# A sum of the down product copied by ScalarE and added by GpSimd, and two attention products put back to their even places

## The chip, the cores and the metric

The kernel runs on one core of a Trainium2 chip. The metric is the device time of one execution in microseconds (us); the number shown is the median of three runs. A core has TensorE (matrix products, PE in the profile, with its weight loads as PEld), VectorE (DVE), ScalarE (ACT), GpSimd (POOL) and SyncE (SP), which here issues the transfers. Each engine has an instruction stream of its own.

## The reference

Everything is in float32. The input x has 2048 tokens of 576 features. A layer norm is followed by two branches that read the same normalised input: a 32-head attention and a gated feed-forward network with 4608 hidden columns. Their results are multiplied and added to x.

```python
x  = A_x                                   # 1 x 2048 x 576
xn = (x - mean) / sqrt(var + 1e-5)
s  = softmax(q k^T * 18**-0.5) v @ wo      # 32 heads of 18, q, k, v = xn @ wqkv
f  = (gelu(xn @ w_gate) * (xn @ w_up)) @ w_down
return x + s * silu(f)
```

## The kernel before, in words

**Sections and rounds.** The feed-forward work is cut into 4 blocks of 512 tokens (index `b`) and 36 groups of 128 hidden columns, so 144 *sections*, run by `section`. Two sections (`g` = 0 and 1) make a *round* `r`, which covers 256 hidden columns; there are 18 rounds in a block. A section makes gate and up sums in one PSUM tile `pgu` from 27 pairs of products (`wh`, `wl` are the high and low halves of a weight, split by GpSimd at lines 118 and 120). ScalarE applies gelu (line 429), VectorE multiplies by the up sum (line 432), and the results `h` are split into `ah` and `al` by GpSimd.

**Attention in the slots.** From section 11 on, a section also carries eight attention *slots*. A slot issues a score product `pe` (line 887), which ScalarE reads with an exponential into `pT` (line 888), and a product `pm` (line 846) that VectorE reduces to row maxima `mx` (line 847) for scores that are needed later. `spread` puts these 16 pairs of products between the 27 pairs of `pgu`, evenly, at places `i * 27 // 16 + 1`. After the section TensorE multiplies `pT` with the values (`acc`, line 904).

**The down product.** After the `g` = 0 section of a round comes the down product of the round before (`downs`, `down`), in a form with seven products instead of eight. Each of the seven sums goes through a PSUM tile `py` (lines 513 to 518). `halved` issues each in two halves, the second one after the first half of the next sum; the last two halves, of the sixth and of the seventh sum, stand next to each other. `take` then adds `py` to the running sum `M[m]`; VectorE does this for all seven (line 568). In the first round of a block (`r` = 0) it is a copy (lines 564 and 566). The order of the seven is `PRODUCTS`, whose last but one entry is `(4, (5, 1))`: it makes `M[4]`, from part 1 of the weight tile `T`.

**The ring.** `pgu`, `pe`, `pm`, `acc` and `py` share a ring of four PSUM tiles of two banks each, given out in turn. `pgu` holds one for the whole section, so the slots go round the other three. With the tiles numbered by the order in which the down product fills them, the fifth, sixth and seventh `py` are followed by the first `pe`, the first `pm` and the second `pe`; after that the second `pm` takes the tile of the first `pe`, the third `pe` that of the first `pm`, the third `pm` that of the second `pe`, and so on.

**Rounds that form T.** `T` holds the weights of the down product, split into high and low halves, in seven combinations. In 18 of the rounds (`FORMED`) it is computed: GpSimd makes the sums `tsum` from the raw weights, ScalarE writes the high halves (`high_b`, lines 488, 490 and 491), GpSimd the low ones (`low_b`, lines 496, 498 and 499), and the result is stored to memory; later rounds load it from there. There is one `T`, so line 488, which writes parts 3 to 6, waits for the first four of the seven products to have read them, line 490 (part 2) for the fifth, and line 491 (parts 0 and 1) for the last.

**What sets the order.** The instruction order of TensorE and of SyncE's queue is that of the program. The scheduler sets the order of the other engines, except for instructions that are held to program order (`keep_in_program_order`).

**LATER.** A section that follows a down product passes `LATER = {1: 1, 4: 1}` to `spread`: entry 1 (the first `pm`) and entry 4 (the third `pe`) of the 16 stand one pair of `pgu` later than their even places.

Of the kernel before, what the change touches and what calls it, by code (L numbers as in the profile page):

```python
# [8 lines left out]
F32 = mybir.dt.float32  # L9
F32R = mybir.dt.float32r  # L10
AF = mybir.ActivationFunctionType
ALU = mybir.AluOpType
# [5 lines left out]
P = 128  # L18
# [14 lines left out]
SLOTS = 8  # L33
# [6 lines left out]
NF = NB * NR * G  # L40
# [5 lines left out]
DC, TH = D // 2, TB // 2  # L46
ENDS = NF - len(FIRST) - NU * NA
# [4 lines left out]
SCALED = G * (NR + PLAIN + 1) - len(FIRST) + 1  # L52
PRODUCTS = ((2, (0, 6)), (5, (1, 3)), (3, (2, 5)), (6, (3, 4)), (0, (4, 2)), (4, (5, 1)), (1, (6, 0)))
SHARED = 8
LATER = {1: 1, 4: 1}
QUARTERS = ((0, 0, 6), (0, 1, 4), (1, 0, 1), (1, 1, 5))
PIECES = ((0, 3, 7), (0, 0, 3), (1, 3, 7), (1, 0, 3))
ADD, SUB = ALU.add, ALU.subtract
# [14 lines left out]
    return ap.bitcast(F32)  # L73


def spread(pairs, specials, first=None, hooks={}, later={}):

    n, m = len(pairs), len(specials)
    at = [-(-(i + 1) * n // m) - 1 if first is None else i * n // m + first + later.get(i, 0) for i in range(m)]
    out = []  # L80
    for i in range(n):
        out += [p for p, j in zip(specials, at) if i == j] + hooks.get(i, [])
        out.append(pairs[i])
    return out
# [3 lines left out]
def kernel(ctx: ExitStack, tc: tile.TileContext, x, wqkv, wo, w_gate, w_up, w_down, out):  # L88
    nc = tc.nc
# [83 lines left out]
    with tc.tile_pool(name="pro", bufs=1) as pro, tc.tile_pool(name="pps", bufs=1, space=PSUM) as pps:  # L173
# [120 lines left out]
        def split_qk(t, raw):  # L294
            hi, lo = (pro.tile([P, KT, P], F32R, name=f"q{m}{t}") for m in "hl")
            first = split(hi, lo, raw)
            put_qk(t, hi, lo)
            return first
# [31 lines left out]
        t = ORDER[0]  # L330
# [24 lines left out]
        for b in range(NB):  # L355
            if b == NB - 1:
                tc.keep_in_program_order(nc.scalar.activation(eps, eps, AF.Tanh))
            for n, t in enumerate(ORDER):
# [4 lines left out]
                if b == 0 and ahead_qk:  # L363
                    first = split_qk(*ahead_qk.pop(0))
# [28 lines left out]
    ffn = ctx.enter_context(tc.tile_pool(name="ffn", bufs=1, reuse_waits="tile"))  # L393
# [3 lines left out]
    FF = {"w": ahead, "xd": XD, "down": [], "gates": [], "n": 0, "hooks": {}, "raw": {},  # L397
          "M": ffn.tile([P, 7, 2, DC], F32, name="M"),
          "A": [ffn.tile([P, 7, TH], F32R, name=m) for m in ("ah", "al")],
          "T": ffn.tile([P, 2, 7, DC], F32R, name="T")}  # L400
# [4 lines left out]
    def ring(name):  # L405

        return ps.tile([P, 2, TB], F32, name=name, tag="ring", bufs=RING)
# [135 lines left out]
    def down_plain():  # L543
        (ah, al), M = FF["A"], FF["M"]
        jobs = []
        for i, c, into in ((0, 0, ((6, ALU.add),)), (0, 1, ((2, ALU.add), (5, ALU.subtract))),
                           (1, 0, ((3, ALU.subtract), (6, ALU.subtract))), (1, 1, ((5, ALU.add),))):

            def add_to(py, into=into):
                for m, op in into:  # L550
                    nc.vector.tensor_tensor(M[:, m], M[:, m], py[:, :, 0:DC], op=op)

            jobs.append(([(h, 2 * g + i, w, 2 * g + c) for g in range(G) for h, w in ((ah, 0), (ah, 1), (al, 0))], add_to))
        halved(jobs)

    def down(b, r, then={}):
        if b == 0 and r < PLAIN:
            return down_plain()
        (ah, al), T, M = FF["A"], FF["T"], FF["M"]

        def take(py, m):
            if r == 0:
                if b == 1:
                    nc.vector.tensor_copy(M[:, m], py[:, :, 0:DC])
                else:
                    nc.scalar.activation(M[:, m], py[:, :, 0:DC], AF.Copy)
            else:
                nc.vector.tensor_tensor(M[:, m], py[:, :, 0:DC], M[:, m], op=ALU.add)  # L568
            for eng, to, op, by in then.get(m, ()):
                eng.tensor_tensor(M[:, to], M[:, to], M[:, by], op=op)  # L570

        terms = ((ah, 0), (ah, 1), (al, 0))
        if FF["n"] < NF - ENDS:
            halved([([(h, i, w, k) for h, w in terms], lambda py, m=m: take(py, m)) for m, (i, k) in PRODUCTS])
        else:
            for m, (i, k) in PRODUCTS:
                py = ring("py")
                for t in range(2):
                    tt = slice(t * P, (t + 1) * P)
                    for n, (h, w) in enumerate(terms):  # L580
                        nc.tensor.matmul(py[:, t, 0:DC], h[:, i, tt], T[:, w, k], start=n == 0, stop=n == 2)  # L581
                take(py, m)
        if r == NR - 1 and b < NB - 1:
            FF["gates"].append(b)
            for k, (p, q) in enumerate(COMBINED):
                combine_at(6 * k + 6, nc.gpsimd, q)
                combine_at(6 * k + 6, nc.gpsimd, p)

    def combine_at(i, eng, what):
        FF["hooks"].setdefault(i, []).append(lambda: combine(eng, *what))  # L590
# [15 lines left out]
        FF["rawd"] = ffn.tile([P, G, D], F32, name="rawd")  # L606
        nc.sync.dma_start(FF["rawd"], w_down[r * G * P:(r + 1) * G * P, :].rearrange("(g p) n -> p g n", p=P))

    def section(specials=(), slots=False, later={}):

        n = FF["n"]
        FF["n"] += 1
        b, r = divmod(n // G, NR)
        g = n % G
        keep = tc.keep_in_program_order
        pairs, pg, pu = gate_up()
        hooks, FF["hooks"] = FF["hooks"], {}

        def hook(i, what):
            hooks.setdefault(i, []).append(what)  # L620

        for i in range(n + 1, min(n + 3, NF)):
            if i not in FF["raw"]:
                FF["raw"][i] = load_gu(gu_part(i))
        nxt = FF["raw"].pop(n + 1, None)
        one = split_ap if n + 1 < ATT.start else split
        if nxt:
            for k in range(NG - 1):
                split_gu(nxt, k, one)
        if n == 0:  # L630
            load_rawd(0)
        if g == 0 and (b, r) in FORMED:
            raw = FF["rawd"]
            hook(12, lambda: sums_b(raw))
        new = n + 1 < NF and (n + 1) % (NR * G) == 0
        xd = []
        if new:
            for k in range(NG - 1):
                hook(9 * k + 9, lambda k=k: xd.append(load_xd(b + 1, k)))
        for p in spread(pairs, specials, 1 if slots else None, hooks, later):  # L640
            p()
        if nxt:
            split_gu(nxt, NG - 1, one)
        if n == 0:
            cut_plain_b(FF["rawd"])
        FF["w"] = nxt
        FF["act"] = activate(pg, pu, g, n)
        if new:
            xd.append(load_xd(b + 1, NG - 1))
            for t in hooks.get(len(pairs), ()):  # L650
                t()
            FF["xd"] = xd

    def downs(then={}):
        done = False
        while FF["down"] and (FF["down"][0][-1] < FF["n"] or FF["n"] == NF):
            down(*FF["down"].pop(0)[:-1], then)
            done = True
        return done

    def finish():

# [123 lines left out]
    with tc.tile_pool(name="att", bufs=1, reuse_waits="tile") as att:  # L786
# [103 lines left out]
        def slot_pairs(s):  # L890

            um, im = divmod(s + LEAD, NS)
            return [lambda: score_pair(*divmod(s, NS))] + [lambda: max_pair(um, im)] * (um < NU)
# [64 lines left out]
            downs()  # L958
            finish()
        scaled = gated = 0  # L960
        later = {}
        for n in range(NU * NA):
            u, i = divmod(n, NA)
            s0 = n * SLOTS
            section([p for s in range(s0, s0 + SLOTS) for p in slot_pairs(s)], True, later)
            load_k(n + KB)
            if i == 1 and u + 2 < NU:
                load_q(u + 2)
            gates()
            tasks(n, 0)  # L970
            if FF["n"] % G == 1 and SCALED <= n < NU * NA - 2 and 2 < FF["n"] % (NR * G) < NR * G - 2:
                done = scaled + gated
                if (scaled + 1) * NA + 4 < n:
                    jobs, k = (load_scale, scale, store_scale), scaled
                    scaled += 1
                else:
                    jobs, k = (load_gate, gate, store_gate), gated
                    gated += 1
                jobs[0](k, done % 2)
                at(n + 2, 0, jobs[1], k, done % 2)  # L980
                at(n + 3, 0, jobs[2], k, done % 2)
            um, im = divmod(s0 + LEAD + SLOTS, NS)
            for kt in range(i * SLOTS // 2, (i + 1) * SLOTS // 2):
                values(u, kt)
            if im == 0 and um <= NU:
                max_parts(um - 1)
            load_v(n + 2)
            tasks(n, 1)
            later = LATER if downs() else {}
            tasks(n, 2)  # L990
            finish()
            for b in range(2):
                if n == NU * NA - NA + 2 * b:
                    load_o(b)
# [3 lines left out]
    with tc.tile_pool(name="epi", bufs=1, reuse_waits="tile") as epi:  # L998
# [7 lines left out]
        n = 0  # L1006
# [133 lines left out]
        first = FF["n"]  # L1140
# [37 lines left out]
        for m in ("rawd", "tsum"):  # L1178
            t = ffn.tile([P, 2, D], F32, name="xxs", tag=m)
# [16 lines left out]
        M = FF["M"]  # L1196
# [17 lines left out]
        for i, c, m in QUARTERS:  # L1214
            t = ffn.tile([P, 2, DC], F32, name="tg", tag=("h0", "h1")[c], bufs=2 - c)
# [34 lines left out]
```

## Time and profile before

| what | value |
|---|---|
| median of three runs | 2529.95 us (2529.44 to 2530.23) |
| the profiled execution: its time | 2528.7 us |
| its span from first to last instruction | 2526.9 us |
| granted TensorE clock, mean | 1.000 |
| busy: TensorE, weight loads, VectorE, ScalarE, GpSimd | 100%, 72%, 75%, 66%, 63% |

The busy time of TensorE overlaps itself, because the products of the two halves of the array run side by side and their ends are modelled; so 100% says that TensorE nearly always has a product under way, not that it runs as densely as it could. Where it loses time is read from the distance between the starts of its products. In the waits, PEld is TensorE's weight load: a wait there is a loss only in so far as the product behind it starts late.

### The profile page before, as it was taken

To read this page: it belongs to the slowest core of one execution; us is meant where nothing else is said; L and a number is where in the kernel's file an instruction comes from. 1 tells how busy PE (TensorE), PEld (TensorE's weight loads), DVE (VectorE), ACT (ScalarE), POOL (GpSimd) and SP (SyncE) were. 2 spreads that over 40 slices of the span, in tenths; PEclk is the share of its full clock that TensorE was granted. 3 is DMA by queue.
4 is the path that set the end of the run, shared out by engine and by line. 5 is a ranking of instruction groups with operands and counts; after the bars stand their busy time and mean duration, and the time that the engine had idled before them with its cause. 6 is when DMAs were issued, how large, how long until landed. Compare 5 with 4: busy or idle time off the path is not lost.

```text
span 2526.9 us, 58757 instructions
## 1 busy us (share of the span) xinstructions
PE 2520.1 (100%) x23434; PEld 1827.4 (72%) x23434; DVE 1890.4 (75%) x2085; ACT 1666.2 (66%) x1889; POOL 1599.4 (63%) x1652
## 2 busy tenths in 40 slices
PE   9999999999999999999999999999999999999999
PEld 8888866666766677666667666676666676666789
DVE  5326788888888888888887888888887788888247
ACT  3223377778777776777777777677777777777731
POOL 3005688888888875666657556566667666666773
PEclk9999999999999999999999999999999999999999
DMA  8965456555585566666677666666668666665766
GB/s 262 313 206 139 120 173 170 153 168 164 170 246 155 165 177 151 167 163 168 169 218 191 175 174 166 169 170 163 156 162 244 167 173 173 172 164 153 190 186 243
DMA packets 416649, 455.40 MB, mean 180 GB/s; under 512 B 109428, under 2 KB 289396, under 8 KB 416376
## 3 DMA queue, kind: packets, MB, share of 16 engines
q1 hardware_dynamic: 416376, 451.64, 65.1%
q8 instruction: 186, 3.05, 0.5%
q14 instruction: 87, 0.71, 0.1%
HBM read 354.38 MB, written 97.13 MB: 179 GB/s over the span
## 4 chain that ended last, share of the span: by engine, by line
PE 97%; DMA 2%; DVE 1%; POOL 0%; issue 0%; SPq 0%; ACT 0%; POOLq 0%; DVEq 0%
PE pgu L420 35%; PE acc L904 18%; PE py L518 16%; PE pm L846 10%; PE pe L887 9%; PE po L194 7%; PE po L1059 1%; DMA raw<-in_B_w_up_dram 1%; PE py L581 1%; PE pt L264 0%; DMA rT<-rec 0%; DMA xx<-in_A_wo_dram 0%; DMA T<-ts 0%; DMA xx<-in_A_x_dram 0%; DVE ol L1042 0%
## 5 line engine op out<-in xcount | busy, mean ns | idle before, releaser
L888 ACT ACTIVATE pT<-pe 128x1024 f32<-128x1024 f32 x1024 | 1048.6, 1027 | 469.4 <-PE pe L887 435.6
L847 DVE TENSOR_REDUCE mx<-pm 128x2 f32<-128x1024 f32 x1024 | 1218.7, 1226 | 143.9 <-PE pm L846 128.8
L420 PE MATMUL pgu<-xd,wh 64*128 64x512 f32 x5184 | 958.5, 393 | 0.0
L420 PEld LDWEIGHTS pgu<-xd,wh 64*128 64x128 f32 x5184 | 496.2, 184 | 122.5 <-issue 41.6
L118 POOL TENSOR_SCALAR wh<-raw 128x384 fp32r<-128x384 f32 x402 | 208.5, 519 | 506.7 <-PE pgu L420 264.0
L420 PE MATMUL pgu<-xd,wl 64*128 64x512 f32 x2592 | 514.4, 390 | 0.2 <-POOL wl L120 0.2
L904 PE MATMUL acc<-pT,VS 128*32 128x512 f32 x4096 | 466.0, 595 | 0.0
L120 POOL TENSOR_TENSOR wl<-raw,wh 128x384 fp32r<-128x384 f32 x402 | 407.4, 1014 | 33.0
L846 PE MATMUL pm<-KA,QT 64*128 64x512 f32 x2048 | 411.9, 396 | 0.2 <-DVE mx L847 0.2
L887 PE MATMUL pe<-QT,KA 64*128 64x512 f32 x2048 | 408.1, 391 | 0.0
L518 PE MATMUL py<-T,ah 64*128 64x288 f32 x3848 | 389.8, 294 | 0.0
L568 DVE TENSOR_TENSOR M<-py,M 128x576 f32<-128x576 f32 x448 | 333.2, 756 | 54.7 <-PE py L518 39.9
L518 PEld LDWEIGHTS py<-T,ah 64*128 64x128 f32 x3848 | 317.6, 184 | 53.2 <-issue 52.8
L441 POOL TENSOR_TENSOR al<-h,ah 128x512 fp32r<-128x512 f32 (+1 forms) x143 | 295.6, 2067 | 49.2 <-ACT ah L438 24.0
L904 PEld LDWEIGHTS acc<-pT,VS 128*32 128x32 f32 x4096 | 120.0, 109 | 276.9 <-issue 229.8
L518 PE MATMUL py<-T,al 64*128 64x288 f32 x1924 | 294.9, 291 | 0.0
L420 PEld LDWEIGHTS pgu<-xd,wl 64*128 64x128 f32 x2592 | 247.6, 184 | 46.6 <-POOL wl L120 0.6
L887 PEld LDWEIGHTS pe<-QT,KA 64*128 64x128 f32 x2048 | 192.9, 184 | 112.0 <-DVE mx L847 12.5
L432 DVE TENSOR_TENSOR h<-h,pgu 128x512 f32<-128x512 f32 x139 | 95.6, 687 | 194.2 <-ACT h L429 190.1
L846 PEld LDWEIGHTS pm<-KA,QT 64*128 64x128 f32 x2048 | 195.1, 184 | 55.5 <-ACT pT L888 15.8
L518 PEld LDWEIGHTS py<-T,al 64*128 64x128 f32 x1924 | 192.2, 185 | 0.0
L429 ACT ACT_TABLE_LOAD x129 | 165.5, 1283 | 2.4
(151 smaller groups left out, 2138.4 us busy)
## 6 DMA issues: line engine op xcount, KB each, us to landing
T<-ts SPq DMA_DIRECT2D x98, 576.0 KB
KA<-qk SPq DMA_DIRECT2D x768, 72.0 KB
T<-ts SPq DMA_DIRECT2D x98, 432.0 KB
raw<-in_B_w_gate_dram SPq DMA_DIRECT2D x144, 288.0 KB
raw<-in_B_w_up_dram SPq DMA_DIRECT2D x144, 256.0 KB
ts<-T SPq DMA_DIRECT2D x36, 576.0 KB
VS<-vs SPq DMA_DIRECT2D x128, 152.0 KB
qk<-t SPq DMA_DIRECT2D x72, 256.0 KB
```

The lines of the kernel that those rows point to most:

```text
L118: first = nc.gpsimd.tensor_scalar(hi, raw, 1.0, 1.0, op0=ALU.mult, op1=ALU.mult)
L120: keep(nc.gpsimd.tensor_tensor(lo, raw, f(hi), op=ALU.subtract))
L194: nc.tensor.matmul(o, st, m, start=(i == 0), stop=(i == len(terms) - 1))
L420: nc.tensor.matmul(o, w[1 + wp][k][rr, c, :], xd[k][xp][rr, c, :], start=(i == 0), stop=(i == len(terms) - 1))
L441: low = two.tensor_tensor(lo, raw, f(hi), op=ALU.subtract)
L518: one = nc.tensor.matmul(py[:, t, 0:DC], h[rr, a, t * P:(t + 1) * P], T[rr, w, k], start=x == 0 and n == 0, stop=x == 1 and n == len(terms ...
L568: nc.vector.tensor_tensor(M[:, m], py[:, :, 0:DC], M[:, m], op=ALU.add)
L846: nc.tensor.matmul(pm[:, a], QS[u, r][rr, t * P:(t + 1) * P], KS[(u * NA + c) % KB][r][rr, :], start=True, stop=True)
L847: nc.vector.tensor_reduce(MX[u][:, 2 * r:2 * r + 2, t, c], pm, axis=AX.X, op=ALU.max)
L887: nc.tensor.matmul(pe[:, a], KS[(u * NA + c) % KB][r][rr, t * P:(t + 1) * P], QS[u, r][rr, :], start=True, stop=True)
L888: nc.scalar.activation(PT[u, kt][:, 2 * r:2 * r + 2, :], pe, AF.Exp, scale=SCALE)
L904: nc.tensor.matmul(ACC[u][32 * a:32 * a + 32, :], VS[(u * NA + c) % VB][:, v:v + 32], pt[:, a, :], start=first, stop=last, skip_group_chec ...
```

## The change

The sixth of a round's seven down sums (`MOVED`, that of `M[4]`) is no longer added by VectorE. ScalarE copies `py` into a tile `msum` in SBUF and GpSimd adds `msum` to `M[4]`. Both instructions are held to program order. This is done where `r > 0` and before the end rounds: 60 rounds. `msum` takes its place from the two buffers of the tag `h0`, which the `h` tiles of the `g` = 0 sections use. `LATER` and what passed it on are removed, so that the first `pm` and the third `pe` of the slots after a down product stand at their even places again.

```diff
-LATER = {1: 1, 4: 1}
+MOVED = PRODUCTS[-2][0]
...
-    at = [-(-(i + 1) * n // m) - 1 if first is None else i * n // m + first + later.get(i, 0) for i in range(m)]
+    at = [-(-(i + 1) * n // m) - 1 if first is None else i * n // m + first for i in range(m)]
...
         def take(py, m):
-            if r == 0:
+            if m == MOVED and r > 0 and FF["n"] < NF - ENDS:
+                t = ffn.tile([P, 2, DC], F32, name="msum", tag="h0", bufs=2)
+                tc.keep_in_program_order(nc.scalar.activation(t, py[:, :, 0:DC], AF.Copy))
+                tc.keep_in_program_order(nc.gpsimd.tensor_tensor(M[:, m], t, M[:, m], op=ALU.add))
+            elif r == 0:
...
-            section([p for s in range(s0, s0 + SLOTS) for p in slot_pairs(s)], True, later)
+            section([p for s in range(s0, s0 + SLOTS) for p in slot_pairs(s)], slots=True)
...
-            later = LATER if downs() else {}
+            downs()
```

The change shows in the instruction streams at two places. The first is a round that forms `T`: ScalarE's stream from the end of the `g` = 0 section (the last of the gelu's instructions, on `one_exp`) to the exponentials of the next section. Before:

```order
L431 ACTIVATE one_exp<-one_exp 128x1
L488 ACTIVATE T<-tsum 128x1152
L490 ACTIVATE T<-tsum 128x288
L491 ACTIVATE T<-rawd 128x576
L888 ACTIVATE pT<-pe 128x1024 x8
```

And now, with the copy at line 564:

```order
L431 ACTIVATE one_exp<-one_exp 128x1
L564 ACTIVATE msum<-py 128x576
L488 ACTIVATE T<-tsum 128x1152
L490 ACTIVATE T<-tsum 128x288
L491 ACTIVATE T<-rawd 128x576
L889 ACTIVATE pT<-pe 128x1024 x8
```

The copy of the sixth sum stands ahead of all three writes of `T`, and these stand ahead of the exponentials. Of the 60 copies, 16 are followed by line 488 in this way; in the other 44 rounds the next instruction is the exponential.

GpSimd's stream in the same kind of round, from the difference that makes `h` of the `g` = 0 section complete to the split of `h`, before:

```order
L449 TENSOR_TENSOR h_7230<-h_7230 128x256
L496 TENSOR_TENSOR T<-tsum,T 128x1152
L498 TENSOR_TENSOR T<-tsum,T 128x288
L499 TENSOR_TENSOR T<-rawd,T 128x576
L440 TENSOR_SCALAR ah<-h_7230 128x512
L441 TENSOR_TENSOR al<-h_7230,ah 128x512
```

And now:

```order
L449 TENSOR_TENSOR h_7244<-h_7244 128x256
L565 TENSOR_TENSOR M<-msum,M 128x576
L496 TENSOR_TENSOR T<-tsum,T 128x1152
L498 TENSOR_TENSOR T<-tsum,T 128x288
L499 TENSOR_TENSOR T<-rawd,T 128x576
L440 TENSOR_SCALAR ah<-h_7244 128x512
L441 TENSOR_TENSOR al<-h_7244,ah 128x512
```

The addition stands ahead of the low halves of `T`. In the other rounds it stands behind the split (line 441), ahead of the next section's weight splits.

The second place is TensorE's stream at the first slots of a section that follows a down product, from the second pair of `pgu` on (the first `pe` is behind the reader). Before:

```order
L420 MATMUL pgu<-xd_0_1008,wl 128x512 x2
L420 MATMUL pgu<-xd_0_1010,wh 128x512 x2
L846 MATMUL pm<-KA,QT_1954 128x512 x2
L420 MATMUL pgu<-xd_0_1008,wh 128x512 x2
L887 MATMUL pe<-QT_1953,KA 128x512 x2
L420 MATMUL pgu<-xd_0_1008,wl 128x512 x2
L420 MATMUL pgu<-xd_0_1010,wh 128x512 x2
L846 MATMUL pm<-KA,QT_1954 128x512 x2
L420 MATMUL pgu<-xd_0_1008,wh 128x512 x2
L420 MATMUL pgu<-xd_0_1008,wl 128x512 x2
L887 MATMUL pe<-QT_1953,KA 128x512 x2
L420 MATMUL pgu<-xd_0_1010,wh 128x512 x2
```

And now:

```order
L420 MATMUL pgu<-xd_0_1008,wl 128x512 x2
L847 MATMUL pm<-KA,QT_1954 128x512 x2
L420 MATMUL pgu<-xd_0_1010,wh 128x512 x2
L420 MATMUL pgu<-xd_0_1008,wh 128x512 x2
L888 MATMUL pe<-QT_1953,KA 128x512 x2
L420 MATMUL pgu<-xd_0_1008,wl 128x512 x2
L420 MATMUL pgu<-xd_0_1010,wh 128x512 x2
L847 MATMUL pm<-KA,QT_1954 128x512 x2
L420 MATMUL pgu<-xd_0_1008,wh 128x512 x2
L888 MATMUL pe<-QT_1953,KA 128x512 x2
L420 MATMUL pgu<-xd_0_1008,wl 128x512 x2
L420 MATMUL pgu<-xd_0_1010,wh 128x512 x2
```

The first `pm` and the third `pe` each moved ahead of one pair of `pgu`; the second `pe` and the second `pm` stayed. VectorE's stream changes only in that the additions of a down product (line 568, now 572) are six in a row instead of seven. SyncE's stream is the same.

More of the change, by code (lines that the diff above doesn't have):

```diff
@@ L73, in f, with spread @@
     return ap.bitcast(F32)
-def spread(pairs, specials, first=None, hooks={}, later={}):
+def spread(pairs, specials, first=None, hooks={}):
     n, m = len(pairs), len(specials)
-    at = [-(-(i + 1) * n // m) - 1 if first is None else i * n // m + first + later.get(i, 0) for i in range(m)]
+    at = [-(-(i + 1) * n // m) - 1 if first is None else i * n // m + first for i in range(m)]
     out = []
@@ L607, in load_rawd, with section @@
         nc.sync.dma_start(FF["rawd"], w_down[r * G * P:(r + 1) * G * P, :].rearrange("(g p) n -> p g n", p=P))
-    def section(specials=(), slots=False, later={}):
+    def section(specials=(), slots=False):
         n = FF["n"]
@@ L639, in section @@
                 hook(9 * k + 9, lambda k=k: xd.append(load_xd(b + 1, k)))
-        for p in spread(pairs, specials, 1 if slots else None, hooks, later):
+        for p in spread(pairs, specials, 1 if slots else None, hooks):
             p()
@@ L654, in downs @@
     def downs(then={}):
-        done = False
         while FF["down"] and (FF["down"][0][-1] < FF["n"] or FF["n"] == NF):
             down(*FF["down"].pop(0)[:-1], then)
-            done = True
-        return done
     def finish():
@@ L960 @@
         scaled = gated = 0
-        later = {}
         for n in range(NU * NA):
```

## Prediction

> **What bounds the kernel.** I read the page first, for the engine that sets the end, then the waits of the weight loads, since only those can hold TensorE up, and then two stretches of the timeline, because a sum over 2527 us mixes rounds of two kinds.
>
> ```profile
> PE 2520.1 (100%) x23434; PEld 1827.4 (72%) x23434; DVE 1890.4 (75%) x2085; ACT 1666.2 (66%) x1889; POOL 1599.4 (63%) x1652
> PE 97%; DMA 2%; DVE 1%; POOL 0%; issue 0%; SPq 0%; ACT 0%; POOLq 0%; DVEq 0%
> PEld acc L904 <- DVE mx L847: 45.3, 123, 0.4
> PEld pm L846 <- ACT pT L888: 15.8, 69, 0.4
> PEld pe L887 <- DVE mx L847: 12.5, 75, 0.2
> PEld pe L887 <- DVE M L568: 9.5, 58, 0.2
> ```
>
> The chain that ended last is TensorE for 97% of the span. So VectorE, ScalarE and GpSimd count only where TensorE waits for them, and all such waits of weight loads for the ring come to 83 us, of which a product hides most. The fourth row is the wait that the change removes; the second and third are those that could grow. Now a round without the forming of T, from its down product (first row) into the next section:
>
> ```profile
> 1525.39 0.54 PE L518 MATMUL py<-T,ah 64*128 64x288 f32 x4
> 1526.88 5.38 DVE L568 TENSOR_TENSOR M<-py,M 128x576 f32<-128x576 f32 x7 [0.66 <-PE py L518]
> 1531.02 0.41 PE L420 MATMUL pgu<-xd,wh 64*128 64x512 f32 x2
> 1531.76 2.13 ACT L888 ACTIVATE pT<-pe 128x1024 f32<-128x1024 f32 x2 [6.28 <-PE pe L887]
> 1532.18 0.41 PE L420 MATMUL pgu<-xd,wh 64*128 64x512 f32 x2
> 1532.32 0.19 PEld L887 LDWEIGHTS pe<-QT,KA 64*128 64x128 f32 x2 [0.16 <-DVE M L568]
> 1532.40 0.42 PE L887 MATMUL pe<-QT,KA 64*128 64x512 f32 x2
> 1532.41 4.74 DVE L847 TENSOR_REDUCE mx<-pm 128x2 f32<-128x1024 f32 x4
> 1532.66 0.39 PE L420 MATMUL pgu<-xd,wl 64*128 64x512 f32 x2
> 1533.81 0.40 PE L887 MATMUL pe<-QT,KA 64*128 64x512 f32 x2
> 1534.31 2.12 ACT L888 ACTIVATE pT<-pe 128x1024 f32<-128x1024 f32 x2 [0.41 <-PE pe L887]
> 1534.53 0.52 POOL L118 TENSOR_SCALAR wh<-raw 128x384 fp32r<-128x384 f32 x1 [4.86 <-PE pgu L420]
> 1535.20 0.40 PE L420 MATMUL pgu<-xd,wh 64*128 64x512 f32 x2
> 1535.38 0.19 PEld L846 LDWEIGHTS pm<-KA,QT 64*128 64x128 f32 x2 [0.22 <-ACT pT L888]
> 1535.43 0.45 PE L846 MATMUL pm<-KA,QT 64*128 64x512 f32 x2
> 1535.72 0.40 PE L420 MATMUL pgu<-xd,wh 64*128 64x512 f32 x2
> ```
>
> A pair of products takes TensorE 0.23 us (1535.20 to 1535.43), so the first `pm` stands at 1531.95, ahead of the pair at 1532.18. There are two losses. The load of the second `pe`, behind VectorE's last addition (it ends at 1526.88 + 5.38 = 1532.26), makes the next pair start 0.26 behind the `pe` (1532.40 to 1532.66): 0.03 lost. The load of the fourth `pm`, behind the exponential of the third `pe`, makes 1535.43 to 1535.72 into 0.29: 0.06 lost. They also give an allowance: loads that began 0.14 and 0.18 behind the start of the pair before cost 0.03 and 0.06, so a load may begin 0.12 behind it for nothing, and each later moment is lost in full.
>
> Now a round that forms T, where the next section begins at 637.61:
>
> ```profile
> 635.90 1.17 ACT L488 ACTIVATE T<-tsum 128x1152 fp32r<-128x1152 f32 x1 [3.83 <-POOL wl L120]
> 636.97 0.43 ACT L490 ACTIVATE T<-tsum 128x288 fp32r<-128x288 f32 x1
> 637.10 1.77 SPq L470 DMA_DIRECT2D ts<-T  x2
> 637.15 2.69 POOL L496 TENSOR_TENSOR T<-tsum,T 128x1152 fp32r<-128x1152 f32 x1 [0.56 <-ACT T L488]
> 637.61 0.41 PE L420 MATMUL pgu<-xd,wh 64*128 64x512 f32 x2
> 637.83 0.69 ACT L491 ACTIVATE T<-rawd 128x576 fp32r<-128x576 f32 x1 [0.43 <-PE py L518]
> 638.42 2.07 ACT L888 ACTIVATE pT<-pe 128x1024 f32<-128x1024 f32 x2
> 639.47 0.40 PE L420 MATMUL pgu<-xd,wh 64*128 64x512 f32 x2
> 639.48 0.19 PEld L846 LDWEIGHTS pm<-KA,QT 64*128 64x128 f32 x2
> 646.92 3.09 SPq L814 DMA_DIRECT2D KA<-qk  x6
> 647.92 0.51 POOL L118 TENSOR_SCALAR wh<-raw 128x384 fp32r<-128x384 f32 x1 [0.79 <-PE pgu L420]
> 650.77 1.28 POOL L452 TENSOR_TENSOR h<-h,h 128x512 f32<-128x512 f32 x1 [1.25 <-DVE h L432]
> 663.04 0.60 ACT L429 ACTIVATE h<-pgu 128x512 f32<-128x512 f32 x1
> ```
>
> Here ScalarE works while the down product is still running: line 488 starts 1.7 us before the section, line 490 follows, and only line 491 has to wait for the last product. The first exponential starts at 638.42 and ends about 639.45, and the load of the second `pm`, which needs the tile of the first `pe`, starts at 639.48 without a wait. So this chain just fits: 0.03 and the allowance of 0.12 to spare.
>
> **The change part by part.** What is added and what it meets, with the mean duration of one in ns behind the comma:
>
> ```profile
> L847 DVE TENSOR_REDUCE mx<-pm 128x2 f32<-128x1024 f32 x1024 | 1218.7, 1226 | 143.9 <-PE pm L846 128.8
> L566 ACT ACTIVATE M<-py 128x576 f32<-128x576 f32 x14 | 8.8, 652 | 4.3 <-POOL wl L120 1.8 <-PE py L518 1.5
> L595 POOL TENSOR_TENSOR M<-M 128x576 f32<-128x576 f32 x24 | 33.4, 1434 | 0.0
> L568 DVE TENSOR_TENSOR M<-py,M 128x576 f32<-128x576 f32 x448 | 333.2, 756 | 54.7 <-PE py L518 39.9 <-PE py L581 3.7
> ```
>
> VectorE loses 60 additions of 0.76 us, 45 us of work, of which TensorE sees only the last addition's end. A down product takes 1531.02 - 1525.39 = 5.63 us for 14 halves, 0.40 each. Line 491 tells when the seventh sum is ready: 0.22 behind the section's start (637.83 against 637.61); the sixth is ready one half earlier, 0.18 ahead of it. In the plain round the last addition can now start at 1531.24 instead of 1531.50 (1532.26 - 0.76) and end at 1532.00. The load of the second `pe`, which would stand at 1532.18, no longer waits: 0.03 back. The first `pm`, one pair earlier, starts at 1531.72 and its reduction, 0.46 behind it as before (1531.95 to 1532.41), at 1532.18. The third `pe`, also one pair earlier (1533.81 - 0.23 = 1533.58), waits for that reduction's tile: 1532.18 + 1.23 + 0.06 for the signal (above, 1532.26 to 1532.32) = 1533.47, and its load may start until 1533.35 + 0.12. It fits exactly. With the third `pe` its exponential comes 0.23 earlier, so the 0.22 wait of the fourth `pm` goes: 0.06 back. Together 0.09 in each of 60 rounds: -5.4 us. The ends: nothing, if the tight fit fails by as much, and half as much again (-8.1), if smaller delays that I can't single out go too.
>
> ScalarE gets 60 copies of 0.65. In the 44 plain rounds it is idle then (6.28 us before the exponential at 1531.76): a copy from 1530.84 to 1531.49 ends 0.27 ahead of it. The first `pm` takes the tile that the copy frees, at 1531.55; its load would stand at 1531.48 and has until 1531.60. No cost.
>
> In the 16 rounds where line 488 follows the copy, ScalarE's stream is in order, so all three writes of T now wait for the sixth sum. The copy starts at 637.61 - 0.18 = 637.43. Line 488 is 1.17 long and line 490 starts 1.07 behind it, so neighbours overlap by 0.10. Then: line 488 at 637.43 + 0.55 = 637.98; line 490 at 639.05; line 491 at 639.38 (0.43 - 0.10); the first exponential 0.59 behind that (638.42 - 637.83), at 639.97 instead of 638.42. It ends at 641.00; with 0.06 for the signal the load of the second `pm` starts at 641.06, 1.59 behind the pair at 639.47. Less the allowance, 1.47 us lost, with nothing to hide it: the pairs of `pgu` behind that `pm` stand in the same stream. It isn't won back either, as TensorE has no slack elsewhere. 16 x 1.47 = +23.5 us. Ends: a copy as short as line 490 (0.43) or as long as VectorE's form (0.76) gives 1.25 to 1.58 each, 20.0 to 25.3 in all.
>
> By the Trainium skill (PSUM — Partial Sum Buffer, Engine vs sequencer instructions) ScalarE's queue is strictly first in, first out, and products of TensorE start in program order. No row of this trace shows an instruction overtaking another; if ScalarE could let line 488 pass the waiting copy, the 23.5 would fall to nearly nothing, which is the first rival below.
>
> GpSimd gets 60 additions of 1.43. In plain rounds it waits 4.86 us until 1534.53, and an addition from 1531.55 to 1532.98 fits into that. In the 16 rounds it stands ahead of line 496, which moves from 637.15 to 638.14 + 1.40 = 639.54, 2.4 later. TensorE itself is 1.47 later by then, and GpSimd waits 0.79 and 1.25 at 647.92 and 650.77 for TensorE and VectorE: 3.5 us of cover against 2.4, so nothing. SyncE's store of T (637.10) is held up with line 488 by 2.1 us; its next issue is at 646.92: nothing. `msum` and `h` share two buffers, so the next gelu of a `g` = 0 section (663.04) waits for the readers of the last one (from 650.77, three operations, some 3 us): 9 us of cover, nothing.
>
> Sum: -5.4 + 23.5 = +18.1 us. On the profiled execution 2528.7 + 18.1 = 2546.8; the median of the runs is 1.25 above that execution, so 2548. With the ends: 20.0 - 8.1 = +11.9 to 25.3 - 0, 2542 to 2555.
>
> **The rivals.**
> - ScalarE's delay is absorbed, and the time falls. Place: the second `pm` of the 16 sections. For it: ScalarE is busy 66% and waits long in plain rounds. Against it: the exponential ends 0.03 before the load wants its tile, and four ring tiles with `pgu` holding one leave no other. It would decide if the first exponential could be 1.5 us later for free. Then -5.4 stays: 2524.6. Chance 0.06.
> - GpSimd becomes late in the 16 rounds. If the two waits of 2.04 us are not there in most of them, 2.4 - 1.47 = 0.93 more is lost in each, +15: 2563. Against it: the waits stand behind the addition in the same round. 0.07.
> - The products at their even places wait for the first reduction again, in all rounds: 0.23 a round, 60 x 0.23 = +13.8: 2562. It decides from 0 us on, the fit being exact, so it may well come in part, which the range holds; in full only if the last addition isn't earlier. 0.06.
> - The longer wait costs TensorE its clock.
>
> ```profile
> PEclk9999999999999999999999999999999999999999
> ```
>
> The granted clock is at full speed in all slices before. If a wait of 1.47 us halved it until the section's end, some 8 us away, each of the 16 would lose 8 more: 2548 + 128 = 2676. Chance 0.01. The Trainium skill (TensorE: Matmul & The Clock Gate, What's actually happening) says that TensorE falls to half clock only after an idle window of about 3.4 us; by that rule this doesn't happen, and no run here shows where the limit lies.
>
> **How the numbers follow.** The likeliest case has 0.76: 2548. Another 0.04 go to its weak form, 16 stalls of under a third of their size (at most 7.8 us, against -5.4): 2525 to 2532. The range, 2540 to 2558, holds its ends (2542 to 2555) and a part of the second and third rival. A measurement of this kernel tells about 0.2% (5 us) from no change. Faster than that: the first rival, 0.06. Within it: the weak form, 0.04. Slower: 0.90.
>
> **What would show it.** Right: in the 16 rounds the first exponential starts about 2.4 us behind the section's start instead of 0.8, the second `pm` waits about 1.5 us for `pT`, and the wait of `pm` for ScalarE's `pT` goes from 15.8 to about 24 us with its longest at 1.5 instead of 0.4, while the wait of `pe` for `M` vanishes. Wrong: no such wait, or waits of `pgu` for `wh` or `wl`, or of `pe` for `mx`, that grow by 10 us or more.

## The result: 21 us slower

| | before | after |
|---|---|---|
| median | 2529.89 us (2529.26 to 2530.48, 6 runs) | 2551.18 us (2550.97 to 2552.10, 6 runs) |
| span of the profiled execution | 2526.9 us | 2549.1 us |
| granted TensorE clock, mean | 1.000 | 1.000 |

The ratio is 1.0085 (1.0072 to 1.0098): 21.3 us more. It is slower, as forecast, and 3 us above the forecast of 2548.

From the page after, the busy time of each engine and the chain of work that ended last:

```profile
PE 2523.1 (99%) x23434; PEld 1862.7 (73%) x23434; DVE 1850.6 (73%) x2025; ACT 1699.5 (67%) x1949; POOL 1680.5 (66%) x1712
PE 95%; ACT 1%; issue 1%; POOL 1%; DVE 0%; DMA 0%; SPq 0%; ACTq 0%; DVEq 0%; POOLq 0%
```

VectorE is 40 us less busy, and the kernel is 21 us slower. ScalarE now has 1% of the chain where it had 0. A percentage so small is easy to pass over, but 1% of 2549 us is some 25 us, of the order of the whole loss. It is rounded, and the chain counts what stands in it and not what was lost, so it tells where to look and not how much. The waits of TensorE after (total us, number, longest; PEld is the weight load, PE the product itself) say more:

```profile
PEld pm L847 <- ACT pT L889: 27.0, 22, 1.6
PE pm L847 <- ACT pT L889: 18.5, 16, 1.2
PEld pe L888 <- DVE mx L848: 10.7, 64, 0.2
PEld pm L847 <- ACT msum L564: 2.7, 14, 0.4
```

Before, the wait of `pm` for `pT` was 15.8 us in 69 pieces of at most 0.4; now it is 27.0 in 22 pieces of at most 1.6, and the products themselves wait as well, 16 times, for 18.5 us. Sixteen is the number of rounds that form T, and each of the 16 lies in the section behind one of them. The wait of `pe` for VectorE's `M` has no row any more: it is gone. That of `pe` for `mx`, 12.5 us before, has not grown. The last row is new: the first `pm` waits for the tile that the copy frees.

**A round that forms T, after.** The timeline (start, us, engine, line; in brackets the idle time before and its releaser), from the copy of the sixth sum on, with TensorE, ScalarE and GpSimd:

```profile
650.07 0.65 ACT L564 ACTIVATE msum<-py 128x576 f32<-128x576 f32 x1 [5.42 <-PE py L518]
650.20 0.39 PE L420 MATMUL pgu<-xd,wh 64*128 64x512 f32 x2
650.62 1.16 ACT L488 ACTIVATE T<-tsum 128x1152 fp32r<-128x1152 f32 x1
651.67 0.43 ACT L490 ACTIVATE T<-tsum 128x288 fp32r<-128x288 f32 x1
652.00 0.67 ACT L491 ACTIVATE T<-rawd 128x576 fp32r<-128x576 f32 x1
652.04 0.44 PE L420 MATMUL pgu<-xd,wh 64*128 64x512 f32 x2
652.19 2.63 POOL L496 TENSOR_TENSOR T<-tsum,T 128x1152 fp32r<-128x1152 f32 x1
652.58 1.93 ACT L889 ACTIVATE pT<-pe 128x1024 f32<-128x1024 f32 x2
653.64 0.18 PEld L847 LDWEIGHTS pm<-KA,QT 64*128 64x128 f32 x2 [1.59 <-ACT pT L889]
653.64 0.50 PE L847 MATMUL pm<-KA,QT 64*128 64x512 f32 x2 [1.17 <-ACT pT L889]
653.98 0.40 PE L420 MATMUL pgu<-xd,wh 64*128 64x512 f32 x2
...
661.74 1.07 PE L905 MATMUL acc<-pT,VS 128*32 128x512 f32 x8
664.75 1.28 POOL L452 TENSOR_TENSOR h<-h,h 128x512 f32<-128x512 f32 x1 [1.08 <-DVE h L432]
```

The section begins at 650.20. ScalarE sits idle for 5.42 us ahead of the copy, because the copy needs a sum that TensorE finishes only then. Behind it come the three writes of T, back to back, and the first exponential starts at 652.58, 2.38 behind the section's start. The second `pm` wants its weights right behind the pair at 652.04; they are loaded at 653.64. It would have started at 652.27, so it is 1.37 late, and the next pair comes 0.34 behind it instead of 0.23: 1.48 lost. Nothing gives it back: from the first pair to the first `acc` product the section takes 661.74 - 650.20 = 11.54 us. The same section before began at 637.61 (shown with the prediction) and ended with the first row of its values on TensorE's timeline:

```profile
647.75 1.07 PE L904 MATMUL acc<-pT,VS 128*32 128x512 f32 x8
```

10.14 us. The 16 sections took 10.10 to 10.18 before and 11.52 to 11.56 after: 16 x 1.40 = 22.4 us, as much as the whole difference of the spans (22.2).

**A plain round, after.** The same view, with the slots' first products:

```profile
1685.35 0.65 ACT L564 ACTIVATE msum<-py 128x576 f32<-128x576 f32 x1 [4.85 <-PE py L518]
1685.46 0.41 PE L420 MATMUL pgu<-xd,wh 64*128 64x512 f32 x2
1685.69 0.76 DVE L572 TENSOR_TENSOR M<-py,M 128x576 f32<-128x576 f32 x1 [0.43 <-PE py L518]
1686.05 0.26 PEld L847 LDWEIGHTS pm<-KA,QT 64*128 64x128 f32 x2
1686.16 0.47 PE L847 MATMUL pm<-KA,QT 64*128 64x512 f32 x2
1686.21 2.17 ACT L889 ACTIVATE pT<-pe 128x1024 f32<-128x1024 f32 x2 [0.21 <-PE pe L888]
1686.66 1.23 DVE L848 TENSOR_REDUCE mx<-pm 128x2 f32<-128x1024 f32 x1 [0.22 <-PE pm L847]
1686.85 0.46 PE L888 MATMUL pe<-QT,KA 64*128 64x512 f32 x2
1687.08 0.46 PE L420 MATMUL pgu<-xd,wl 64*128 64x512 f32 x2
1687.77 0.47 PE L420 MATMUL pgu<-xd,wh 64*128 64x512 f32 x2
1687.94 0.19 PEld L888 LDWEIGHTS pe<-QT,KA 64*128 64x128 f32 x2
1688.01 0.48 PE L888 MATMUL pe<-QT,KA 64*128 64x512 f32 x2
1688.28 0.44 PE L420 MATMUL pgu<-xd,wl 64*128 64x512 f32 x2
1689.89 0.44 PE L847 MATMUL pm<-KA,QT 64*128 64x512 f32 x2
1690.13 0.43 PE L420 MATMUL pgu<-xd,wh 64*128 64x512 f32 x2
```

Here the copy holds up nothing on ScalarE: its next instruction is the exponential at 1686.21, which waits for its `pe`, not for the copy. The pair behind the second `pe` is 0.23 behind it (1686.85 to 1687.08; 0.26 before), the one behind the fourth `pm` 0.24 (1689.89 to 1690.13; 0.29 before). These are the two gains that were forecast. But the pair behind the third `pe` is now 0.27 behind it (1688.01 to 1688.28): VectorE's first reduction ends at 1687.89, the third `pe` loads at 1687.94, 0.17 behind the pair at 1687.77, and 0.04 is lost. Over the plain rounds the section's median went from 10.15 to 10.12 us, so some 0.04 is left of the 0.09 that were forecast (0.02 and 0.06 won, 0.04 lost).

### The profile page after: what moved, and what is told of

The parts are those of the page before. It is cut to its first block, busy times and chain, and to the rows that moved or that the text cites. A ratio compares the mean times of both kernels' runs of the same rounds, so it can differ in the third digit from the quotient of the medians.

```text
span 2549.1 us, 58908 instructions
## 1 busy us (share of the span) xinstructions
PE 2523.1 (99%) x23434; PEld 1862.7 (73%) x23434; DVE 1850.6 (73%) x2025; ACT 1699.5 (67%) x1949; POOL 1680.5 (66%) x1712
## 4 chain that ended last, share of the span: by engine, by line
PE 95%; ACT 1%; issue 1%; POOL 1%; DVE 0%; DMA 0%; SPq 0%; ACTq 0%; DVEq 0%; POOLq 0%
PE pgu L420 34%; PE acc L905 18%; PE py L518 15%; PE pm L847 9%; PE pe L888 9%; PE po L194 7%; PE po L1059 2%; PE py L585 1%; ACT pT L889 1%; ACT T L491 0%; PE pt L264 0%; ACT T L490 0%; POOL wl L120 0%; ACT T L488 0%; DMA xx<-in_A_x_dram 0%
## 5 line engine op out<-in xcount | busy, mean ns | idle before, releaser
L420 PEld LDWEIGHTS pgu<-xd,wh 64*128 64x128 f32 x5184 | 518.3, 184 | 111.7 <-issue 42.4
L420 PE MATMUL pgu<-xd,wl 64*128 64x512 f32 x2592 | 524.6, 390 | 0.0
L847 PE MATMUL pm<-KA,QT 64*128 64x512 f32 x2048 | 421.8, 396 | 18.8 <-ACT pT L889 18.5
L888 PE MATMUL pe<-QT,KA 64*128 64x512 f32 x2048 | 418.7, 392 | 0.0
L572 DVE TENSOR_TENSOR M<-py,M 128x576 f32<-128x576 f32 x388 | 293.3, 757 | 79.0 <-PE py L518 65.8
L420 PEld LDWEIGHTS pgu<-xd,wl 64*128 64x128 f32 x2592 | 257.8, 184 | 39.4 <-POOL wl L120 0.3
L847 PEld LDWEIGHTS pm<-KA,QT 64*128 64x128 f32 x2048 | 207.7, 184 | 68.4 <-ACT pT L889 27.0
L564 ACT ACTIVATE msum<-py 128x576 f32<-128x576 f32 x60 | 39.1, 651 | 320.1 <-PE py L518 294.1
```

The source lines that it names most:

```text
L420: nc.tensor.matmul(o, w[1 + wp][k][rr, c, :], xd[k][xp][rr, c, :], start=(i == 0), stop=(i == len(terms) - 1))
L847: nc.tensor.matmul(pm[:, a], QS[u, r][rr, t * P:(t + 1) * P], KS[(u * NA + c) % KB][r][rr, :], start=True, stop=True)
L888: nc.tensor.matmul(pe[:, a], KS[(u * NA + c) % KB][r][rr, t * P:(t + 1) * P], QS[u, r][rr, :], start=True, stop=True)
```

## The experiments

The theory: what costs is the place of the copy in ScalarE's stream in 16 rounds. It waits for the sixth sum, and three writes of T and the exponentials wait behind it. Rivals: A, the two products at their even places; B, the work itself, a copy and an addition in each of 60 rounds; C, GpSimd's addition ahead of line 496. The first four runs shared a kernel before of 2529.24 us (27 runs), the last three one of 2529.60 (13 runs). A place "S+0.94" is 0.94 us behind the section's first pair of `pgu`.

**1. The sum moved, the products left late.** This tells A from the rest.

```diff
 LATER = {1: 1, 4: 1}
+MOVED = PRODUCTS[-2][0]
...
-            if r == 0:
+            if m == MOVED and r > 0 and FF["n"] < NF - ENDS:
+                ...
+            elif r == 0:
```

> The sixth sum moves to ScalarE and GpSimd as in the change, but the two products stay at their late places. Theory (in the 16 rounds that form T the copy stands ahead of ScalarE's writes of T and makes the first exponentials 1.5 us late): nearly the whole loss stays, 16 x 1.4 to 1.5 = 22 to 24 us, about 2552 us, and the first exponential of those sections starts 2.3 to 2.4 us behind the section's start. Rival A (the loss comes from the two products at their even places): no loss, 2528 to 2530 us.

Measured: 2552.28 us, 1.0091 (1.0077 to 1.0105), and in the waits

```profile
PE pm L851 <- ACT pT L893: 19.3, 16, 1.2
```

The loss is all there without the two products' move, so A doesn't carry it.

**2. The products at their even places alone.** VectorE still adds all seven sums.

```diff
-LATER = {1: 1, 4: 1}
+LATER = {}
```

> Only the two products go to their even places; VectorE adds all seven sums. Theory: a loss of its own, since the first reduction is as late as before and the third product of scores waits 0.2 us for it in some 63 sections, 10 to 13 us, about 2541 us; the first exponential of the 16 sections stays at 0.8 us. Rival A (the even places are the change's loss): about 2551 us, with the loss in the 16 rounds.

Measured: 2530.98 us, 1.0007 (0.9999 to 1.0016). I had expected 10 to 13 us, and 1.7 came (by the interval -0.3 to 4.0). Its timeline, in a section that begins at 1499.60:

```profile
1498.63 2.21 DVE L568 TENSOR_TENSOR M<-py,M 128x576 f32<-128x576 f32 x3
1500.23 0.25 PEld L846 LDWEIGHTS pm<-KA,QT 64*128 64x128 f32 x2 [0.20 <-DVE M L568]
1500.31 0.48 PE L846 MATMUL pm<-KA,QT 64*128 64x512 f32 x2
1500.57 0.69 PE L420 MATMUL pgu<-xd,wh 64*128 64x512 f32 x4
1500.83 1.23 DVE L847 TENSOR_REDUCE mx<-pm 128x2 f32<-128x1024 f32 x1
```

I had taken VectorE's last addition for what holds the first reduction up, since before the one ends at 1532.26 and the other starts at 1532.41. Here the addition ends at 1500.84 and the reduction starts at 1500.83, at S+1.23; before it was at S+1.39. So the late place of the first `pm` had set it, and with the product earlier the reduction moves up by 0.16 of the 0.23, until the addition stops it. That leaves small costs: this `pm` loads late behind the sixth addition, and the next pair comes 0.26 behind it instead of 0.23 (0.05 over at the median of these sections); 0.04 goes at the third `pe`. Against them stand 0.06 back at the fourth `pm` and 0.02 at the second `pe`. The two places are worth next to nothing either way.

**3. The sum moved in the plain rounds only.** In the 16 rounds that form T VectorE adds it as before.

```diff
+        def forming():
+            n = FF["n"] - 1
+            return n >= ATT.start and n % G == 0 and divmod(n // G, NR) in FORMED
...
-            if m == MOVED and r > 0 and FF["n"] < NF - ENDS:
+            if m == MOVED and r > 0 and FF["n"] < NF - ENDS and not forming():
```

> As the change, but in the 16 rounds that form T VectorE adds the sixth sum again; 44 rounds keep the move, all products stand at their even places. Theory: the 1.4 us in each of the 16 rounds go, and these rounds pay 0.2 us for the even places without the relief, 3 to 4 us in all; about 2533 us. Rival B (the loss is the added work of ScalarE and GpSimd, in proportion to the number of sums moved): 44 / 60 of 21 us stay, about 2545 us.

Measured: 2529.12 us, 0.9999 (0.9991 to 1.0008). With 44 of the 60 copies and additions still moved, the loss is gone. B is out: the work costs nothing that the runs can tell where nothing but the exponential stands behind it. The 3 to 4 us that I had expected for the even places did not come, for the reason that the second experiment gives.

**4. The writes of T first, then the copy.** All 60 sums are moved, and every instruction is that of the changed kernel. In the 16 rounds lines 488 and 490 are issued behind the fourth and the fifth sum, so that the copy stands between 490 and 491.

```diff
     def high_b(part):
         if part == 0:
             keep(nc.scalar.activation(T[:, 0, 3:7], t[:, 1:5], AF.Copy))
-        else:
+        if part == 1:
             keep(nc.scalar.activation(T[:, 0, 2], t[:, 0], AF.Copy))
+        if part == 2:
             keep(nc.scalar.activation(T[:, 0, 0:2], q[:, 0:4:3], AF.Copy))
...
         def take(py, m):
...
+            if m in (PRODUCTS[3][0], PRODUCTS[4][0]) and forming():
+                high_b((PRODUCTS[3][0], PRODUCTS[4][0]).index(m))
...
-                    high_b(0)
-                    high_b(1)
+                    high_b(2)
```

> As the change, with all 60 sums moved, but in the rounds that form T ScalarE's first two writes of T stand ahead of the copy, and only the third behind it. The same instructions, in another order. Theory: the first exponential starts at about 1.0 us behind the section's start instead of 2.3, which costs 0.1 us or less a round; about 2530 us (2528 to 2533). Rival B (the added work, wherever it stands): about 2551 us. Rival C (GpSimd's addition ahead of the low halves of T): it still stands among them, so most of the loss stays, over 2540 us.

Measured: 2527.31 us, 0.9991 (0.9982 to 1.0000). Its timeline of ScalarE in a round that forms T, the section's first pair of `pgu` among it, and a line of its waits:

```profile
800.86 1.17 ACT L488 ACTIVATE T<-tsum 128x1152 fp32r<-128x1152 f32 x1 [3.83 <-issue]
801.93 0.43 ACT L490 ACTIVATE T<-tsum 128x288 fp32r<-128x288 f32 x1
802.39 0.65 ACT L569 ACTIVATE msum<-py 128x576 f32<-128x576 f32 x1
802.58 0.39 PE L420 MATMUL pgu<-xd,wh 64*128 64x512 f32 x2
802.94 0.67 ACT L492 ACTIVATE T<-rawd 128x576 fp32r<-128x576 f32 x1
803.51 1.93 ACT L895 ACTIVATE pT<-pe 128x1024 f32<-128x1024 f32 x2
```

```profile
PEld pm L853 <- ACT pT L895: 5.1, 24, 0.4
```

Line 488 starts 1.72 ahead of the section again, as before the change, and the first exponential at S+0.93 instead of S+2.38. The wait of the products is gone. I had expected 2528 to 2533 us; it came out just below. The changed kernel was 21.3 us above its kernel before and this one is 1.9 below, so the same instructions in another order are worth some 23 us. GpSimd's addition comes in another place too: it starts at 805.52, behind two of the three low halves of T. So this run alone doesn't tell ScalarE's order from GpSimd's; the seventh does. This is the version to keep if any: against the kernel before it gains 1.9 us, and the interval ends at no change, so a gain is not shown.

**5 and 6. An earlier sum moved.** The copy stays ahead of line 488, but it takes the fifth or the fourth sum instead of the sixth, so it waits 0.8 or 1.6 us less. Both keep `LATER`, so they are to be set beside the first experiment.

```diff
-MOVED = PRODUCTS[-2][0]
+MOVED = PRODUCTS[-3][0]
```

> As the move alone (both products at their late places), but the fifth of the seven sums is moved instead of the sixth. Its copy can start 0.84 us earlier. Theory (what counts is when the sum that the copy waits for is ready): the first exponential of the 16 sections starts at 1.5 us behind the section's start instead of 2.3, the loss there falls from 1.47 to about 0.64 us, 16 x 0.64 = 10 us; about 2540 us. Rival B (the added work): 2552 us as with the sixth sum.

```diff
-MOVED = PRODUCTS[-2][0]
+MOVED = PRODUCTS[-4][0]
```

> The same with the fourth sum, which is ready 1.6 us before the sixth. Theory: the copy and the first two writes of T are done before the last product ends, the third write still starts 0.22 us behind the section's start and the first exponential at 0.8; no loss, 2528 to 2531 us. Rival B (the added work): 2552 us.

Measured: 2540.35 us, 1.0044 (1.0029 to 1.0059) with the fifth, and 2529.83, 1.0001 (0.9992 to 1.0011) with the fourth. The first rows are from the fifth's timeline in a round that forms T, the section's first pair and the first exponential, and a line of its waits; the others from the fourth's timeline at the same place:

```profile
811.53 0.41 PE L421 MATMUL pgu<-xd,wh 64*128 64x512 f32 x2
813.13 1.93 ACT L893 ACTIVATE pT<-pe 128x1024 f32<-128x1024 f32 x2
```

```profile
PE pm L851 <- ACT pT L893: 6.5, 16, 0.4
```

```profile
803.20 0.39 PE L421 MATMUL pgu<-xd,wh 64*128 64x512 f32 x2
804.00 2.05 ACT L893 ACTIVATE pT<-pe 128x1024 f32<-128x1024 f32 x2
```

The exponential starts at S+2.39 with the sixth sum (first experiment), S+1.60 with the fifth and S+0.80 with the fourth, where it was before any change; the time above the kernel before is 23.0, 10.8 and 0.2 us. The first step of 0.79 us in 16 rounds is 12.6 us, and 12.2 were measured: the loss follows the start of the exponential. The Trainium skill (PSUM — Partial Sum Buffer, Engine vs sequencer instructions) has ScalarE's queue as strictly first in, first out. These runs agree: behind the waiting copy no write of T started, though its inputs were there.

**7. GpSimd's 16 additions left out.** In the rounds that form T the copy is made, and the addition of `msum` to `M[4]` is missing, so these terms are missing in the output.

```diff
-                tc.keep_in_program_order(nc.gpsimd.tensor_tensor(M[:, m], t, M[:, m], op=ALU.add))
+                if not forming():
+                    tc.keep_in_program_order(nc.gpsimd.tensor_tensor(M[:, m], t, M[:, m], op=ALU.add))
```

> As the change, with ScalarE's copies at the same places, but GpSimd leaves out the 16 additions of the rounds that form T (these terms are missing from the output). Theory (ScalarE's order alone): nothing changes, about 2551 us. Rival C (GpSimd's addition ahead of the low halves of T makes later work late): the loss goes in good part, under 2543 us.

Measured: 2550.09 us, 1.0083 (1.0067 to 1.0100). From its timeline in a round that forms T, and its waits:

```profile
819.33 0.66 ACT L568 ACTIVATE msum<-py 128x576 f32<-128x576 f32 x1 [5.42 <-PE py L518]
821.11 2.64 POOL L496 TENSOR_TENSOR T<-tsum,T 128x1152 fp32r<-128x1152 f32 x1 [5.57 <-ACT T L488]
821.84 1.01 ACT L894 ACTIVATE pT<-pe 128x1024 f32<-128x1024 f32 x1
```

```profile
PE pm L852 <- ACT pT L894: 18.3, 16, 1.2
```

GpSimd is free now and idle for 5.57 us, and line 496 still has to wait for line 488; the exponential is as late as ever, 2.51 behind the copy. The 16 sections take 11.52 us in the median, as against 11.54 with the additions. C is out: the loss is not GpSimd's.

## Why the prediction was right, step by step

**The 16 rounds (+23.5).** Right in mechanism and size. Forecast: the first exponential at S+2.36, the load of the second `pm` 1.59 behind the pair before it, 1.47 lost. Measured: S+2.38, 1.60 (652.04 to 653.64), and 1.48. The copy started 0.13 ahead of the section where 0.18 had been worked out from line 491, and it cost 0.55 on ScalarE (650.07 to 650.62), as taken. With the small gains of the same sections the net was forecast at 1.47 - 0.09 = 1.38 and is 1.40. The fourth experiment shows it from the other side.

**VectorE's part (-5.4).** The sign was right, the size not. The two gains came as forecast, and VectorE's last addition started at S+0.23 (forecast 0.22). The step that failed is "It fits exactly": the reduction starts 0.50 behind its `pm` and not 0.46 (1686.16 to 1686.66), so the third `pe` loads 0.17 behind the pair before it, where 0.12 is free, and 0.04 is lost in each round. In the 44 plain rounds that leaves 0.04 each by the medians, 1.8 us instead of 4.0. Behind this stands a cost that had been set at nothing, the copy's effect on the first `pm`: that `pm` waits for the tile that the copy frees, its load starts at 1686.05, 0.05 behind the copy's end, and the load of its second half follows 0.07 later (0.26 for both, 0.19 for one). The fourth experiment shows the link within one run. In its plain rounds the copy ends at S+0.54 and the reduction starts 0.50 behind the `pm` (medians); in its 16 other rounds the copy ends at S+0.48, the reduction starts 0.46 behind the `pm`, and nothing is lost at the third `pe` (the second `pm` makes the pair before it 0.04 late there, but without that too the load would be 0.12 behind the pair). The allowance itself held: 0.14 cost 0.03, 0.17 cost 0.04, 0.18 cost 0.06.

**The costs set at nothing.** ScalarE's copies in plain rounds: confirmed by the third experiment within its noise, but for the 0.04 a round just named. GpSimd in the 16 rounds: line 496 moved to S+1.99 from 0.46 ahead of the section, 2.4 later as forecast, and it then works until 663.67 without a wait that the profile shows. Of the two waits that were to cover this, that of 0.79 us is used up and the other is still there (1.08 at 664.75, for VectorE): it caught up before the next `h`. The seventh experiment agrees.

Two of the plain rounds lost time that nothing in the forecast covers. This timeline row of the changed kernel is from one of them:

```profile
2280.85 0.65 ACT L564 ACTIVATE msum<-py 128x576 f32<-128x576 f32 x1 [5.13 <-POOL al L441]
```

Its section began at 2280.68, so the copy started 0.17 behind it instead of 0.12 ahead, and the section took 10.40 us, 0.3 more than its like. The profile names GpSimd's line 441 as what released it. That is not the whole cause: in the other round the copy, at 1090.10, was as late, though line 441 had ended at 1088.59. The copies of the same two rounds are also late, by some 0.28, in the first, fifth and sixth experiments, and not in the third, fourth and seventh; the cause is open. Two such rounds are 0.6 us.

**The rivals.** The delay wasn't absorbed (16 waits of 1.2 us in the products). GpSimd's lateness is refuted by the seventh experiment, and the wait at the even places by the first two: its price of 0.23 a round was taken from a reduction that I thought VectorE held up, and it is some 0.04. The clock stayed at 1.000 through sixteen waits, in which the products paused for at most 1.2 us. By the Trainium skill (TensorE: Matmul & The Clock Gate, What's actually happening) it falls only after an idle window of about 3.4 us; this trace agrees.

**What is left.** Added up section by section over the two profiled executions, the 16 sections took 22.5 us more and the 44 plain ones 0.8 less, the two late ones included. The sections that the change doesn't touch, those that follow a product with the values alone, took 0.8 more, some 0.01 each. That is 22.5 against 22.2 of the spans. In the experiments these untouched sections took 0.2 to 1.0 us more than before, the most in the second, which moves no sum; so this is not a property of the moved sum, and its cause is open. The 3 us by which the forecast was low are in the main the plain rounds: -0.8 instead of -4.0, where 0.6 of the difference are the two late copies and the rest the smaller gain.

## What to carry to other kernels

When work is given to an engine with time to spare, look at what stands behind the new instruction in that engine's stream, and at when its input is ready: a copy of 0.65 us that waits for a late sum delayed everything behind it by 1.5 us, on an engine that was idle for 5.4 us ahead of it. If instructions whose inputs are ready earlier stand behind it, issue them first; the same instructions in another order were worth some 23 us. A chain that "fits exactly" should be costed as a small loss, since the row from which its delay is read was measured in another arrangement.

## What the runs showed of the hardware

- TensorE takes a weight load that begins up to about 0.12 us behind the start of the pair before it without any loss; beyond that the delay is lost in full, from 0.14 (0.03 lost) up to 1.60 (1.48 lost). Counted over the score products of the slots in the trace before, 28 loads that began 0.12 behind cost nothing in the median, and 33 that began 0.19 behind cost 0.06 each.
- Neighbouring instructions of ScalarE overlap: line 488 takes 1.16 us and the next starts 1.05 behind it, the copy takes 0.65 and the next starts 0.55 behind it. A chain on ScalarE is shorter by 0.1 us for each link than the sum of its durations.
